# Retention two chunks at a time in a fused retention and maxout-FFN kernel

## The chip, the cores and the metric

The kernel runs on one core of a Trainium2 chip. The metric is device time in microseconds (us) of one execution; the figure given is the median of several runs. Engines are named as in the profile: PE is TensorE (matmul), PEld its weight loads, DVE is VectorE, ACT is ScalarE, POOL is GpSimd, SP is the queue that issues nearly all DMAs.

## The reference

The first half is retention, attention without a softmax: for 8 batches of 8 heads, 576 positions and 64 features,

```
scores = q @ k.T / sqrt(64)
ret    = scores * gamma_head ** (i - j)      (zero where j > i)
x      = ret @ v
```

with one gamma per head. The heads are put side by side, so x has 4608 rows of 512. The second half is a maxout FFN: h = max(x @ w1, x @ w2, x @ w3) with 768 hidden columns, and out = h @ w_out, 4608 x 512. q, k, v are float32; the weights come as 64-bit floats and are turned into float32 on the chip.

## The kernel before, in words

The 4608 rows are cut into 36 chunks of 128 rows (C) and 9 tiles of 512 rows (four chunks each, CPT). A batch has 576 rows, 4.5 chunks, so chunks 4, 13, 22 and 31 hold the end of one batch in their first 64 rows and the start of the next in the last 64; `start_of(g)` gives the row at which a new batch starts in chunk g, or None.

Retention goes by chunk. The decay is split into a factor for the keys (put on v by `decay_values`, on POOL), one for the queries (put on at the end), and a state that carries the earlier chunks of the same batch. For each chunk g there are these steps:

- `load(g)`: q, k and v from memory, all from SP. From chunk 7 on (BY_PE) q and a second copy of k (`kx`) are brought in blocks of 32 x 32 by 16 small DMAs each, so that VectorE's 32 x 32 transpose finishes the job; before that, q and k come whole and are transposed on PE. k and v in plain layout are one DMA each (two where the chunk crosses a batch).
- `transposes(g)` gives kT and qT, heads on partitions in pairs.
- `scores(g)`: 8 matmuls (L186), each with one head's 64 rows of the array, into two PSUM banks; VectorE masks them into `st` (L189). Then, still in `scores`, the state for the next chunk: 4 matmuls of k by decayed v (`kv`, L197), in chunks with a batch start at row 64 with those last 64 rows only; VectorE adds the old state (L200, L202) and POOL multiplies by the decay of a chunk (L203).
- `values(g)`: 8 matmuls of v by `st` (L216), each writing 64 partitions, then 4 of the state by qT (L221) into the same bank `o`, if the chunk has rows that continue a batch; VectorE applies the queries' decay on the way into `xT` (L223). After a tile's fourth chunk it and POOL also make the sums S that the FFN needs (L228 to L231).

[...] four in the ring `ps_r` (tag "r": kt, qt, scores, kv, o, in order of use), two in `ps_x` and two in `ps_y`.

The FFN (`ffn`) is a generator that yields after a unit. In tile 0 a unit is two plain matrix products (`up_plain`, L504), and between them the weights are converted by VectorE, ACT and POOL, step by step (`convert`); each converted piece issues the load of the piece six later (`load_weights`, L258 to L263) on SP, since six raw buffers exist. From tile 1 on a unit is `up`, seven products of half-size blocks (a Strassen-Winograd scheme, L446) with copies on ACT and sums on VectorE; nine units fill h, and `downs` (L319) makes the output in three further stretches, with four stores on SP (L333).

No scheduler reorders anything[...]. The main loop (L576 to L587) interleaves: for tile t, the twelve pieces of the FFN alternate with the steps of the four chunks of tile t + 1, one step before each piece: transposes (and, before it, the load of chunk g + 1), scores (and `decay_values(g + 1)`), values; then the next chunk. Chunks 0 to 3 are done in a prologue (L553 to L573).

Of the kernel before, what the change touches and what calls it, by code (L numbers as in the profile page):

```python
# [34 lines left out]
FP32 = mybir.dt.float32  # L35
# [4 lines left out]
ALU = mybir.AluOpType  # L40
PSUM = bass.MemoryType.PSUM

C = 128
NT = 4 * C
NH = NT // 2
BY_PE = 7
# [5 lines left out]
def kernel(  # L52
# [14 lines left out]
    nc = tc.nc  # L67
    P = 128
    B, H, S, D = q.shape
    N, DM = out.shape  # L70
    DF = moe_w1.shape[1]
    NP = H // 2
    NG = B * S // C
    NDC = DM // P
    NF = DF // P
    CPT = NT // C
# [3 lines left out]
    raw = ctx.enter_context(tc.tile_pool(name="raw", bufs=AHEAD + 1))  # L80
    vpool = ctx.enter_context(tc.tile_pool(name="vpool", bufs=3))
    att = ctx.enter_context(tc.tile_pool(name="att", bufs=2))
    stp = ctx.enter_context(tc.tile_pool(name="stp", bufs=2))
    xpool = ctx.enter_context(tc.tile_pool(name="xpool", bufs=2))
    spool = ctx.enter_context(tc.tile_pool(name="spool", bufs=1))
    hpool = ctx.enter_context(tc.tile_pool(name="hpool", bufs=1))
# [5 lines left out]
    ps_r = ctx.enter_context(tc.tile_pool(name="ps_r", bufs=4, space=PSUM))  # L92
# [5 lines left out]
    gq = const.tile([P, NP, C], FP32, name="gq")  # L98
# [17 lines left out]
    def start_of(g):  # L116
        r = -g * C % S
        return r if r < C else None

    masks = {0: causal, None: causal}  # L120
    for r in sorted({start_of(g) for g in range(NG)} - {0, None}):
        m = masks[r] = const.tile([C, C], FP32, name=f"causal{r}")
# [4 lines left out]
    raws, vds, qks, sts, states = {}, {}, {}, {}, {}  # L127

    def spans(g):

        row = 0
        while row < C:
            b, pos = divmod(g * C + row, S)
            n = min(C - row, S - pos)
            yield row, b, pos, n
            row += n

    def load(g, *between):
        rows = (("k", k), ("q", q), ("v", v)) if g < BY_PE else (("k", k), ("v", v))
        for n, src in () if g < BY_PE else (("q", q), ("kx", k)):  # L140

            t = raws[n, g] = raw.tile([P, NP, C // 32, 32], FP32, tag=n, name=n + "raw", bufs=3 if n == "q" else 2)
            for blk in range(C // 32):
                b, pos = divmod(g * C + 32 * blk, S)
                for a in range(4):
                    nc.sync.dma_start(
                        t[32 * a:32 * a + 32, :, blk, :],
                        src[b, a // 2::2, pos:pos + 32, 32 * (a % 2):32 * (a % 2) + 32].rearrange("p j i -> j p i"))
        for n, src in rows:
            if n == "v":  # L150
                for t, what in between:
                    nc.sync.dma_start(t[:], what)
            t = raws[n, g] = raw.tile([C, H, D], FP32, tag=n, name=n + "raw", bufs=4 if n == "k" else 3)
            for row, b, pos, m in spans(g):
                nc.sync.dma_start(t[row:row + m], src[b, :, pos:pos + m, :].rearrange("h p d -> p h d"))

    def decay_values(g):
        t = vds[g] = vpool.tile([C, H, D], FP32, tag="vd", name="vd")
        nc.gpsimd.tensor_tensor(t[:], raws.pop(("v", g))[:], gk[:].unsqueeze(2).to_broadcast([C, H, D]),  # L159
                                op=ALU.mult)  # L160

    def pair(t, p):
        return t[:, 2 * p:2 * p + 2, :].rearrange("a h d -> a (h d)")

    def transposes(g):
        both = qks[g] = {}
        if g >= BY_PE:
            for n in ("k", "q"):
                t = both[n] = att.tile([P, NP, C], FP32, tag=n + "T", name=n + "T", bufs=2 if n == "k" else 3)
                nc.vector.transpose(t[:].rearrange("a p c -> a (p c)"),  # L170
                                    raws.pop(("kx" if n == "k" else n, g))[:].rearrange("a p b i -> a (p b i)"))
            return
        for n, src in (("k", raws["k", g]), ("q", raws.pop(("q", g)))):
            pt = ps_r.tile([P, NP, C], FP32, tag="r", name=n + "t")
            for p in range(NP):
                nc.tensor.transpose(pt[:, p, :], pair(src, p), ident[:C, :C])
            t = both[n] = att.tile([P, NP, C], FP32, tag=n + "T", name=n + "T", bufs=2 if n == "k" else 3)
            nc.scalar.copy(t[:], pt[:])

    def scores(g):  # L180
        qT, kT = qks[g]["q"], qks[g]["k"]
        s = [ps_r.tile([C, NP, C], FP32, tag="r", name=f"s{j}") for j in range(2)]
        for p in range(NP):
            for j in range(2):
                r = slice(D * j, D * (j + 1))
                nc.tensor.matmul(s[j][:, p, :], lhsT=kT[r, p, :], rhs=qT[r, p, :], start=True, stop=True)  # L186
        st = sts[g] = att.tile([C, 2, NP, C], FP32, tag="st", name="st", bufs=2)
        for j in range(2):
            nc.vector.tensor_tensor(st[:, j], s[j][:], masks[start_of(g)][:].unsqueeze(1).to_broadcast([C, NP, C]),  # L189
                                    op=ALU.mult)  # L190
        kr = raws.pop(("k", g))
        if g + 1 == NG or start_of(g + 1) == 0:
            return
        r = start_of(g) or 0
        kv = ps_r.tile([P, NP, P], FP32, tag="r", name="kv")
        for p in range(NP):
            nc.tensor.matmul(kv[:, p, :], lhsT=pair(kr, p)[r:], rhs=pair(vds[g], p)[r:], start=True, stop=True)  # L197
        t = states[g + 1] = stp.tile([P, NP, P], FP32, tag="state", name="state")
        if start_of(g) is not None:
            nc.vector.tensor_tensor(t[:], kv[:], gs[:], op=ALU.mult)  # L200
        else:
            nc.vector.tensor_tensor(t[:], kv[:], states[g][:], op=ALU.add)  # L202
            nc.gpsimd.tensor_tensor(t[:], t[:], gs[:], op=ALU.mult)  # L203

    xT, xS = {}, {}

    def values(g):
        old = C if start_of(g) is None else start_of(g)
        t, i = divmod(g, CPT)
        if i == 0:  # L210
            xT[t] = xpool.tile([P, NDC, NT], FP32, tag="xT", name="xT")
        st, vr, qT = sts.pop(g), vds.pop(g), qks.pop(g)["q"]
        o = ps_r.tile([P, NP, C], FP32, tag="r", name="o")
        for p in range(NP):
            for j in range(2):
                nc.tensor.matmul(o[D * j:D * (j + 1), p, :], lhsT=vr[:, 2 * p + j, :], rhs=st[:, j, p, :],  # L216
                                 start=(p == 0), stop=(old == 0 and p == NP - 1), skip_group_check=True)
        if old > 0:
            sd = states.pop(g)
            for p in range(NP):  # L220
                nc.tensor.matmul(o[:, p, :old], lhsT=sd[:, p, :], rhs=qT[:, p, :old],  # L221
                                 start=False, stop=(p == NP - 1), skip_group_check=True)
        nc.vector.tensor_tensor(xT[t][:, :, i * C:(i + 1) * C], o[:], gq[:], op=ALU.mult)  # L223
        if i == CPT - 1 and t > 0:
            x = xT[t]
            a11, a12, a21, a22 = (x[:, 2 * d:2 * d + 2, NH * r:NH * (r + 1)] for r in range(2) for d in range(2))
            s1, s2, s3, s4 = (spool.tile([P, 2, NH], FP32, tag=f"S{n}", name=f"S{n}") for n in (1, 2, 3, 4))
            nc.vector.tensor_tensor(s1[:], a21, a22, op=ALU.add)  # L228
            nc.vector.tensor_tensor(s2[:], s1[:], a11, op=ALU.subtract)
            nc.gpsimd.tensor_tensor(s3[:], a11, a21, op=ALU.subtract)  # L230
            nc.gpsimd.tensor_tensor(s4[:], a12, s2[:], op=ALU.subtract)  # L231
            xS[t] = {1: a11, 2: a12, 3: s4[:], 4: a22, 5: s1[:], 6: s2[:], 7: s3[:]}
# [200 lines left out]
    def convert(n):  # L433
        for _ in range(n):
            next(converting, None)
# [119 lines left out]
    warm(2)  # L555
    decay_values(1)
    scores(0)
    transposes(1)
    values(0)
    decay_values(2)  # L560
    scores(1)
    transposes(2)
    values(1)
    decay_values(3)
    scores(2)
    transposes(3)
    convert(2)
    values(2)
    convert(2)
    scores(3)  # L570
    decay_values(4)
    convert(2)
    values(3)  # L573
    transposes(4)
    convert(4)
    for t in range(N // NT):  # L576
        work = ffn(t)
        for g in range((t + 1) * CPT, (t + 2) * CPT):
            for step in (transposes, scores, values):
                if g < NG:  # L580
                    if step is transposes and g + 1 < NG:
                        load(g + 1)
                    if step is scores and g + 1 < NG:
                        decay_values(g + 1)
                    if g > CPT or step is not transposes:
                        step(g)
                next(work, None)  # L587


# [49 lines left out]
```

## Time and profile before

| what | value |
|---|---|
| median of 13 runs | 830.18 us (828.86 to 834.15) |
| profiled execution, its own time | 829.92 us |
| its span | 828.2 us |
| PE busy | 822.5 us |
| DVE, POOL, ACT busy | 432.4, 190.4, 173.7 us |
| retention matmuls: scores L186, values L216, state L221, kv L197 | 41.8, 39.8, 36.9, 36.6 us of listed time |
| small q and kx DMAs | 464 each, 16 KB |

The span is the program's own stretch of the trace, about 1.7 us shorter than the execution's time. A group's listed time counts overlapping instructions in full, so the four retention rows add up to more than the stretch they fill. Every matmul stands in the trace as two records. In the chain of waits each record is charged from the end of the one before it to its own end, so its lengths add up to elapsed time.

### The profile page before, as it was taken

The numbers are of one execution on the slowest core, as the hardware profiler recorded it, in microseconds if no ns is written. First come the engines' busy times: TensorE is split into PE (matmuls) and PEld (weight loads), VectorE is DVE, ScalarE is ACT, GpSimd is POOL, SyncE is SP. The second block draws the span as 40 slices with busy tenths as digits, with TensorE's granted clock in tenths as the row PEclk, the third lists the DMA queues.
The fourth block names the chain that finished last, engine by engine and source line by source line (L and its number), as shares of the span: only waits on it lengthen the run. The fifth ranks groups of instructions, "written<-read, shape, count | busy, mean of one in ns | idle before, by whom it ended". The sixth has DMA issues, their size and how long they took to land.

```text
span 828.2 us, 12659 instructions
## 1 busy us (share of the span) xinstructions
PE 822.5 (99%) x4616; PEld 668.7 (81%) x4616; DVE 432.4 (52%) x805; ACT 173.7 (21%) x401; POOL 190.4 (23%) x182
## 2 busy tenths in 40 slices
PE   9999999999999999999999999999999999999998
PEld 8555547888888888888888888888888888888887
DVE  4999886455455544544454445444544435433342
ACT  3766511111111111110111111111111011111211
POOL 3644565212111120113011211111111202101000
PEclk9999999999999999999999999999999999999999
DMA  9964431343133323332233323341333233201001
GB/s 236 296 173 152 103 71 45 57 79 63 51 56 55 57 79 57 56 57 57 56 62 70 62 53 57 56 78 60 56 58 54 59 71 63 46 13 39 1 1 51
DMA packets 236094, 59.33 MB, mean 72 GB/s; under 512 B 217088, under 2 KB 234496, under 8 KB 236032
## 3 DMA queue, kind: packets, MB, share of 16 engines
q1 hardware_dynamic: 235888, 58.53, 31.4%
q8 instruction: 36, 0.59, 0.3%
q14 instruction: 26, 0.21, 0.1%
q10 hardware_dynamic: 144, 0.00, 0.0%
HBM read 49.03 MB, written 9.44 MB: 71 GB/s over the span
## 4 chain that ended last, share of the span: by engine, by line
PE 88%; DVE 5%; issue 2%; ACT 2%; DMA 1%; POOL 0%; SPq 0%; DVEq 0%; ACTq 0%
PE x L446 30%; PE z L446 15%; PE dx L319 10%; PE y L446 8%; PE dz L319 5%; PE s L186 4%; PE o L216 4%; PE kv L197 4%; PE o L221 4%; PE dy L319 3%; PE down L495 2%; DVE expo L398 1%; DVE frac L387 1%; DVE expo L382 1%; DVE mant L393 1%
## 5 line engine op out<-in xcount | busy, mean ns | idle before, releaser
L446 PE MATMUL x<-S,T 128*128 128x256 f32 x576 | 148.0, 379 | 0.0
L159 POOL TENSOR_TENSOR vd<-vraw,gk 128x512 f32<-128x512 f32 x36 | 38.3, 1063 | 364.2 <-DMA vraw<-in_v_dram 358.0
L446 PEld LDWEIGHTS x<-S,T 128*128 128x128 f32 x576 | 109.0, 190 | 15.6 <-ACT u L451 0.3
L446 PE MATMUL x<-xT,w 128*128 128x256 f32 x288 | 74.8, 382 | 0.0
L476 DVE TENSOR_TENSOR tmp<-x,p 128x256 f32<-128x256 f32 x48 | 20.4, 425 | 103.5 <-PE x L446 103.5
L446 PE MATMUL x<-S,w 128*128 128x256 f32 x288 | 74.3, 381 | 0.0
L446 PE MATMUL z<-S,w 128*128 128x256 f32 x288 | 73.9, 379 | 0.0
L446 PE MATMUL z<-xT,T 128*128 128x256 f32 x288 | 73.9, 379 | 0.0
L446 PE MATMUL y<-xT,w 128*128 128x256 f32 x288 | 73.9, 379 | 0.0
L451 ACT COPY p<-x 128x256 f32<-128x256 f32 x72 | 26.8, 372 | 220.2 <-PE x L446 220.2
L189 DVE TENSOR_TENSOR st<-s,causal 128x512 f32<-128x512 f32 x72 | 46.3, 685 | 41.6 <-PE s L186 41.6
L504 PE MATMUL up<-xT,w 128*128 128x512 f32 x144 | 63.5, 594 | 0.2 <-POOL w L404 0.2
L446 PEld LDWEIGHTS z<-S,w 128*128 128x128 f32 x288 | 54.7, 190 | 7.4
L446 PEld LDWEIGHTS y<-xT,w 128*128 128x128 f32 x288 | 54.7, 190 | 7.4
L446 PEld LDWEIGHTS z<-xT,T 128*128 128x128 f32 x288 | 54.5, 189 | 7.7
L223 DVE TENSOR_TENSOR xT<-o,gq 128x512 f32<-128x512 f32 x36 | 24.9, 691 | 68.0 <-PE o L221 61.5
L446 PEld LDWEIGHTS x<-S,w 128*128 128x128 f32 x288 | 49.3, 189 | 13.3 <-issue 1.5
L446 PEld LDWEIGHTS x<-xT,w 128*128 128x128 f32 x288 | 51.5, 190 | 6.6 <-issue 0.8
L297 POOL TENSOR_TENSOR H<-h 128x256 f32<-128x256 f32 x24 | 18.0, 749 | 148.0 <-DVE h L489 148.0
L504 PEld LDWEIGHTS up<-xT,w 128*128 128x128 f32 x144 | 26.7, 190 | 30.7 <-issue 29.9
L465 DVE TENSOR_TENSOR tmp<-y,p 128x256 f32<-128x256 f32 x48 | 20.4, 425 | 52.8 <-PE y L446 52.8
L451 ACT COPY u<-x 128x256 f32<-128x256 f32 x72 | 26.8, 372 | 100.1 <-PE x L446 95.8
(92 smaller groups left out, 1229.2 us busy)
## 6 DMA issues: line engine op xcount, KB each, us to landing
bits<-in_moe_w_dram SPq DMA_DIRECT2D x18, 512.0 KB, 5.1
out_dram<-osb SPq DMA_DIRECT2D x35, 256.0 KB, 2.1
kraw<-in_k_dram SPq DMA_DIRECT2D x32, 256.0 KB, 3.0
vraw<-in_v_dram SPq DMA_DIRECT2D x32, 256.0 KB, 3.4
qraw<-in_q_dram SPq DMA_DIRECT2D x464, 16.0 KB, 1.8
kxraw<-in_k_dram SPq DMA_DIRECT2D x464, 16.0 KB, 1.8
bits<-in_moe_w_out_dram SPq DMA_DIRECT2D x6, 512.0 KB, 3.9
qraw<-in_q_dram SPq DMA_DIRECT2D x6, 256.0 KB, 4.6
```

What stands on the lines that cost most here:

```text
L159: nc.gpsimd.tensor_tensor(t[:], raws.pop(("v", g))[:], gk[:].unsqueeze(2).to_broadcast([C, H, D]), op=ALU.mult)
L186: nc.tensor.matmul(s[j][:, p, :], lhsT=kT[r, p, :], rhs=qT[r, p, :], start=True, stop=True)
L189: nc.vector.tensor_tensor(st[:, j], s[j][:], masks[start_of(g)][:].unsqueeze(1).to_broadcast([C, NP, C]), op=ALU.mult)
L197: nc.tensor.matmul(kv[:, p, :], lhsT=pair(kr, p)[r:], rhs=pair(vds[g], p)[r:], start=True, stop=True)
L216: nc.tensor.matmul(o[D * j:D * (j + 1), p, :], lhsT=vr[:, 2 * p + j, :], rhs=st[:, j, p, :], start=(p == 0), stop=(old == 0 and p == NP - ...
L221: nc.tensor.matmul(o[:, p, :old], lhsT=sd[:, p, :], rhs=qT[:, p, :old], start=False, stop=(p == NP - 1), skip_group_check=True)
L223: nc.vector.tensor_tensor(xT[t][:, :, i * C:(i + 1) * C], o[:], gq[:], op=ALU.mult)
L319: nc.tensor.matmul(out[m], lhsT=hS[n](fp)[:, m * P:(m + 1) * P], rhs=late["T"][n][:, fp, :], start=first and fp == 0 and (m == 0 or last a ...
L446: nc.tensor.matmul(out[:], lhsT=w[:, d * P:(d + 1) * P], rhs=xS[t][n][:, d, :], start=first and d == 0, stop=d == 1, skip_group_check=True)
L451: nc.scalar.copy(c[:], src[:])
L465: nc.vector.tensor_tensor(c11, y[:], p1[:], op=ALU.add)
L504: nc.tensor.matmul(ps[:], lhsT=w_sb[i, fb][:, dc * P:(dc + 1) * P], rhs=xT[t][:, dc, :], start=(dc == 0), stop=(dc == NDC - 1))
```

## The change

`scores` is split: the state part becomes a step `state(g)` of its own. `values` takes several chunks: first the L216 matmuls of all of them, then the L221 matmuls of each with its read-out. `stp`, the ring of states, has three buffers instead of two. `load` gets a part `load_blocks` that issues the small DMAs of chosen blocks of a chunk.

The main loop is replaced by a table of twelve steps, `steps(t)`. From the second of these tables on, chunks a and b go together: transposes of a and the load of a + 2; transposes of b; scores of a and of b in a row and the load of b + 2; state of a; state of b; values of a and b; then the same for the next two. For chunks 4 to 7, which run beside the first tile's FFN and its weight conversion, the table is written out: scores 4 and state 4 stay together between the first two units, scores 5 stand alone, values 4 and 5, scores 6 and 7, values 6 and 7 are in a row, and the small DMAs of chunks 7, 8 and 9 are spread over the steps in blocks.

```diff
-    stp = ctx.enter_context(tc.tile_pool(name="stp", bufs=2))
+    stp = ctx.enter_context(tc.tile_pool(name="stp", bufs=3))
...
-    def load(g, *between):
-        rows = (("k", k), ("q", q), ("v", v)) if g < BY_PE else (("k", k), ("v", v))
-        for n, src in () if g < BY_PE else (("q", q), ("kx", k)):
-
-            t = raws[n, g] = raw.tile([P, NP, C // 32, 32], FP32, tag=n, name=n + "raw", bufs=3 if n == "q" else 2)
-            for blk in range(C // 32):
+    def load_blocks(g, *blocks):
+        for n, src in (("q", q), ("kx", k)):
+
+            if 0 in blocks:
+                raws[n, g] = raw.tile([P, NP, C // 32, 32], FP32, tag=n, name=n + "raw", bufs=3 if n == "q" else 2)
+            t = raws[n, g]
+            for blk in blocks:
...
+    def load(g, *between):
+        if g >= BY_PE and ("q", g) not in raws:
+            load_blocks(g, *range(C // 32))
+        for n, src in (("k", k), ("q", q), ("v", v)) if g < BY_PE else (("k", k), ("v", v)):
...
+    def state(g):
+
         kr = raws.pop(("k", g))
         if g + 1 == NG or start_of(g + 1) == 0:
             return
...
+    def values(*chunks):
+
+
+        def before(g):
+            return C if start_of(g) is None else start_of(g)
+
+        o = {g: ps_r.tile([P, NP, C], FP32, tag="r", name="o") for g in chunks}
+        for g in chunks:
+            st, vr = sts.pop(g), vds.pop(g)
             for p in range(NP):
-                nc.tensor.matmul(o[:, p, :old], lhsT=sd[:, p, :], rhs=qT[:, p, :old],
-                                 start=False, stop=(p == NP - 1), skip_group_check=True)
-        nc.vector.tensor_tensor(xT[t][:, :, i * C:(i + 1) * C], o[:], gq[:], op=ALU.mult)
+                for j in range(2):
+                    nc.tensor.matmul(o[g][D * j:D * (j + 1), p, :], lhsT=vr[:, 2 * p + j, :], rhs=st[:, j, p, :],
+                                     start=(p == 0), stop=(before(g) == 0 and p == NP - 1), skip_group_check=True)
+        for g in chunks:
+            t, i = divmod(g, CPT)
+            qT, old = qks.pop(g)["q"], before(g)
+            if old > 0:
+                sd = states.pop(g)
+                for p in range(NP):
+                    nc.tensor.matmul(o[g][:, p, :old], lhsT=sd[:, p, :], rhs=qT[:, p, :old],
+                                     start=False, stop=(p == NP - 1), skip_group_check=True)
+            if i == 0:
+                xT[t] = xpool.tile([P, NDC, NT], FP32, tag="xT", name="xT")
+            nc.vector.tensor_tensor(xT[t][:, :, i * C:(i + 1) * C], o[g][:], gq[:], op=ALU.mult)
...
+    def steps(t):
...
+        if t == 1:
+            a, b, c, d = range(CPT, 2 * CPT)
+            at(0, (load, b))
+            at(1, (scores, a), (state, a))
+            at(2, (transposes, b), (decay_values, b), (load, c))
+            at(3, (scores, b), (load_blocks, d, 0))
+            at(4, (state, b), (load_blocks, d, 1, 2))
+            at(5, (values, a, b), (load_blocks, d, 3), (load, d))
+            at(6, (transposes, c), (decay_values, c), (load_blocks, d + 1, 0))
+            at(7, (transposes, d), (decay_values, d), (load_blocks, d + 1, 1, 2))
+            at(8, (scores, c), (scores, d), (load_blocks, d + 1, 3), (load, d + 1))
+            at(9, (state, c), (load_blocks, d + 2, 0, 1))
+            at(10, (state, d), (load_blocks, d + 2, 2))
+            at(11, (values, c, d), (load_blocks, d + 2, 3), (load, d + 2))
+            return todo
+        for n in range(0, CPT, 2):
+            a, b, m = CPT * t + n, CPT * t + n + 1, 6 * (n // 2)
+            at(m, (transposes, a), (decay_values, a), (load, a + 2))
+            at(m + 1, (transposes, b), (decay_values, b))
+            at(m + 2, (scores, a), (scores, b), (load, b + 2))
+            at(m + 3, (state, a))
+            at(m + 4, (state, b))
+            at(m + 5, (values, a, b))
+        return todo
+
     for t in range(N // NT):
         work = ffn(t)
-        for g in range((t + 1) * CPT, (t + 2) * CPT):
-            for step in (transposes, scores, values):
-                if g < NG:
-                    if step is transposes and g + 1 < NG:
-                        load(g + 1)
-                    if step is scores and g + 1 < NG:
-                        decay_values(g + 1)
-                    if g > CPT or step is not transposes:
-                        step(g)
-                next(work, None)
+        for todo in steps(t + 1):
+            for step in todo:
+                step()
+            next(work, None)
```

In the prologue each `scores(g)` is followed by `state(g)`, which leaves its order as it was.

More of the change, by code (lines that the diff above doesn't have):

```diff
@@ L148, in load @@
                         src[b, a // 2::2, pos:pos + 32, 32 * (a % 2):32 * (a % 2) + 32].rearrange("p j i -> j p i"))
-        for n, src in rows:
+    def load(g, *between):
+        if g >= BY_PE and ("q", g) not in raws:
+            load_blocks(g, *range(C // 32))
+        for n, src in (("k", k), ("q", q), ("v", v)) if g < BY_PE else (("k", k), ("v", v)):
             if n == "v":
@@ L205 @@
     xT, xS = {}, {}
[L207 to L219, printed above, removed]
-            for p in range(NP):
-                nc.tensor.matmul(o[:, p, :old], lhsT=sd[:, p, :], rhs=qT[:, p, :old],
-                                 start=False, stop=(p == NP - 1), skip_group_check=True)
-        nc.vector.tensor_tensor(xT[t][:, :, i * C:(i + 1) * C], o[:], gq[:], op=ALU.mult)
+    def values(*chunks):
[4 more added lines that the diff above has]
+            st, vr = sts.pop(g), vds.pop(g)
+            for p in range(NP):
+                for j in range(2):
[12 more added lines that the diff above has]
+            nc.vector.tensor_tensor(xT[t][:, :, i * C:(i + 1) * C], o[g][:], gq[:], op=ALU.mult)
         if i == CPT - 1 and t > 0:
@@ L557 @@
     scores(0)
+    state(0)
     transposes(1)
@@ L561 @@
     scores(1)
+    state(1)
     transposes(2)
@@ L565 @@
     scores(2)
+    state(2)
     transposes(3)
@@ L570 @@
     scores(3)
+    state(3)
     decay_values(4)
@@ L575, with at @@
     convert(4)
+    def steps(t):
+        todo = [[] for _ in range(3 * CPT)]
+        def at(n, *what):
+            todo[n].extend(partial(step, *args) for step, *args in what if args[0] < NG)
+        if t == 1:
[22 more added lines that the diff above has]
+        return todo
     for t in range(N // NT):
         work = ffn(t)
-        for g in range((t + 1) * CPT, (t + 2) * CPT):
-            for step in (transposes, scores, values):
-                if g < NG:
-                    if step is transposes and g + 1 < NG:
-                        load(g + 1)
-                    if step is scores and g + 1 < NG:
-                        decay_values(g + 1)
-                    if g > CPT or step is not transposes:
-                        step(g)
-                next(work, None)
+        for todo in steps(t + 1):
+            for step in todo:
+                step()
+            next(work, None)
 _INS = ['q', 'k', 'v', 'moe_w1', 'moe_w2', 'moe_w3', 'moe_w_out']
```

## The prediction

> **What bounds the kernel now.** I read the page first, then TensorE's waits, then the chain of waits in a middle tile, then the queues of the first tile.
>
> ```profile
> PE 822.5 (99%) x4616; PEld 668.7 (81%) x4616; DVE 432.4 (52%) x805; ACT 173.7 (21%) x401; POOL 190.4 (23%) x182
> ...
> PE 88%; DVE 5%; issue 2%; ACT 2%; DMA 1%; POOL 0%; SPq 0%; DVEq 0%; ACTq 0%
> ```
>
> TensorE is busy for 822.5 of 828.2 us. Who waits for whom, TensorE alone, is short:
>
> ```profile
> PE o L216 <- DVE st L189: 0.6, 2, 0.4
> PE s L186 <- ACT qT L178: 0.2, 1, 0.2
> PE up L504 <- POOL w L404: 0.2, 1, 0.2
> ```
>
> With 2.6 us of waits in all, no earlier load and no other buffer can win much: only less work on TensorE can. So I asked what each block costs, from the chain in 300 to 345 us (start, length, instruction, records; a matmul has two records):
>
> ```profile
> 299.95 0.34 PE o L221 x3
> ...
> 314.16 1.09 PE s L186 x16
> 315.25 1.09 PE kv L197 x8
> 316.34 0.86 PE x L446 x4
> ...
> 322.38 1.02 PE o L216 x16
> 323.41 1.09 PE o L221 x8
> 324.50 0.87 PE x L446 x4
> ...
> 336.59 1.09 PE s L186 x16
> 337.68 1.06 PE x L446 x4
> 338.74 0.86 PE y L446 x4
> ```
>
> The FFN's four records take 0.86. Straight after scores (337.68, a chunk with no kv) the same four take 1.06: 0.20 more. After kv (316.34) they take 0.86, but kv itself takes 1.09 for 8 records where the steady pitch of such records is 0.34/3 = 0.112, so 0.90: 0.19 more. Leaving the scores costs about 0.195, whoever comes next. Entering them costs as much: cut at 337.2 us, the chain gives 0.64 for the first 7 score records, so 0.45 for the last 9, four pairs and a bit, 0.112 a pair; eight pairs are 0.90 and the block took 1.09, so 0.195 went to the entry. Likewise L216: 0.47 for its first 5 records, 0.55 for the last 11, 0.109 a pair, 0.87 in all, so 0.15 for the entry; and L221 behind it pays 0.19 for leaving. One chunk's retention pays 0.39 around its scores and 0.345 around its values.
>
> Scores use 64 rows of the array and L216 64 columns, everything else 128x128. The test is a chunk whose kv has 64 rows too (chunk 13, in 244 to 252 us):
>
> ```profile
> 246.82 1.09 PE s L186 x16
> 247.91 0.89 PE kv L197 x8
> 248.81 1.06 PE x L446 x4
> ```
>
> Here kv pays nothing after the scores, and the FFN block behind it pays the 0.20. The price is for changing the shape of the tile.
>
> [...] my blocks run from end to end, and all lengths but those at a change of shape repeat to 0.01 us, so I use them.
>
> **The change, part by part.** *Scores in a row, values in a row.* In tiles 1 to 7 chunks 8 to 35 form 14 pairs; of chunks 4 to 7 the values pair twice and the scores once (6, 7). That is 15 merged score blocks and 16 merged value blocks. Each merge takes away one entry and one exit: 15 x 0.39 = 5.85 us and 16 x 0.345 = 5.5 us. No other record goes or comes. The seam inside a merged block (scores of one chunk, then of the next) isn't in the trace of before. Bounds: a gain has no source, since the pitch inside a block is already steady[...]. I take 0, since the shape stays.
>
> *States on their own.* kv now stands between FFN units; with 128 rows its shape is theirs and it costs 8 x 0.112. But chunks 13, 22 and 31 cross a batch after 64 rows: their kv was next to the scores and shared their shape, and now changes shape twice more: 3 x 0.39 = 1.2 us lost. Chunk 4 also has 64 rows, but its scores and state stay together.
>
> *Four score banks at once.* They take all four ps_r buffers. Two of them last held the values of the pair before, read by VectorE three units (18 us) earlier; the kv one unit later needs a bank whose mask is done. Masks: four at 0.69 listed, about 2.5 us with their overlap. They start when the first chunk's scores end, 0.9 us before the second's, so they end some 1.7 us into the next unit, when its y (0.2 + 2 x 0.86) is just ready for VectorE; even 1 us late they are covered, as the next matmul that needs VectorE in that unit is product 3, five products on. VectorE is busy for 42 of 88 us in such a tile. Cost 0; without the cover up to 2.5 us a pair. The two read-outs of values in a row (2 x 0.69) hide in the same way, and at a tile's end under the four products (10 us) that still follow; GpSimd's S sums end there 6 us or more before they are used now (392.8 against 400).
>
> *Loads two chunks ahead.* SP issues the 34 DMAs of a chunk in 17.5 us (16 for q in about 8.2, 16 for k in 8.4, then 0.4 and 0.5), four chunks in 70 us of a tile of 88, and then waits for the stores (from 379.68 to 397.12 in that tile). SP's order inside a tile stays: four loads, four stores. k's transposed-load buffers are two, so chunk a + 2 can be loaded only when a is transposed, which is done at that same step; SP reaches those DMAs 8 us later, behind q's. In the tile's third load this may be a wait of 1 to 2 us; what stands behind it are loads due three units on and stores whose buffer is wanted 10 us later. Cost 0. As before, stores pace SP, and lag doesn't pile up: loads and four issues (2.5 us) are 73 of a tile of 86.5.
>
> *The first tile.* Here weights are converted on VectorE and SP also brings the weights:
>
> ```profile
> 68.89 8.86 SPq L260 DMA_DIRECT2D bits<-in_moe_w_out_dram  x4
> 77.87 8.58 SPq L146 DMA_DIRECT2D qraw<-in_q_dram  x16
> 86.50 7.55 SPq L146 DMA_DIRECT2D kxraw<-in_k_dram  x16
> ...
> 95.25 1.40 SPq L260 DMA_DIRECT2D bits<-in_moe_w_out_dram  x2
> ```
>
> The last two w_out pieces are queued behind chunk 7's 32 small DMAs; VectorE idles 2.48 us for them at 98.5, and the first down block takes 6.08 us where the second takes 5.32: 0.76 of stall. The change puts chunk 7's loads ahead of them in blocks of 8 and 16, mostly where SP was waiting for freed weight buffers (61.6 to 76.2 us), and only one block of chunk 8 (8 DMAs, 4.3 us) just before these two, so they leave at about 83 to 85 and land by 91. VectorE loses its 2.48 of idling, but before the last conversion it now does chunk 7's transposes (1.4) and masks (1.3) and no longer chunk 6's state add (0.7): 0.5 earlier in all, so the last w_out is there at 108.9 instead of 109.4. TensorE comes to it with 0.9 more (scores of 7) and 0.35 less (values of 4 and 5): it wants the last piece at 104.65 + 0.55 + 10 x 0.43 = 109.5. No stall: 0.76 gained. Bounds: that, and, if the DMAs stay late and VectorE ends 2.0 later, a stall of 1.8, so 1.1 lost. SP carries chunk 9's loads here too, 17.5 us, in time freed at 97 to 116.
>
> Sum: -5.85 - 5.5 + 1.2 - 0.76 = -10.9 us. The profiled execution took 829.92 (span 828.2 and 1.7 around it), 0.26 below the median of 830.18: 829.92 - 10.9 = 819.0, and in terms of the median 819.2.
>
> **The rivals.** [...] 5.6 back, 824.8. For it: nothing shown. Against: inside a block the matmuls already change bank and row half at 0.11 a pair. This is also the case in which the change doesn't do what it says. *The first tile takes some back:* w_out or VectorE late by 2 to 3 us, with the masks of two chunks and chunk 7's transposes in a stretch where VectorE is 100% busy (62 to 83 us): 821 to 822. Against: from the fifth matmul group on weights stand ready 5 to 14 us before use and the PSUM buffers 8. *The banks bind, slower:* the second chunk's scores wait for VectorE to read the banks of the values before, or the next unit waits behind four masks. It decides from 10.9/14 = 0.78 us a pair; with a full pair of masks (1.29) exposed in 15 pairs it would be 819.2 + 19.4 = 838.6. Against: the 18 us between the values and the next scores.
>
> **How the numbers follow.** Chances: forecast 0.70, with its own range 817 to 821 (the medians' noise, some tenths to 1 us, and pitches off by 0.02); first tile 0.12; seam 0.12; banks 0.05; the rest 0.01. From 816.5 to 823 lie the forecast nearly whole and the first tile: 0.8. A no-change within 0.2% (1.7 us) would need the gain lost almost exactly: 0.02. Slower: the banks, 0.05. Faster: 0.93.
>
> **What would show it.** Right: score groups of 32 records in about 1.99 us and value groups of 32 in about 1.9; kv with 128 rows 0.90 and, thrice, 64-row kv with 0.39 around it; TensorE's waits no longer than now; tiles of 86.5 where they were 88; the first down block at 5.2. Wrong: any wait of TensorE for masks or values in tiles 1 to 7, a jump at the 17th record of a merged block, waits of VectorE for q or k loads, or weight waits in the first 110 us.

## The result and the profile after

The changed kernel takes 820.36 us (median of 7 runs, 820.01 to 820.62) against 830.51 us (32 runs) for the kernel before: 0.9874 of it, 95% interval 0.9861 to 0.9886, so 1.3% or about 10.2 us faster. The profiled execution took 820.62, its span 818.9 where it was 828.2.

On the page, TensorE is as full as it was, but busy for 10.2 us less with the same 4616 records. So the price of the changes of shape had stood in its busy time, not in its idle time:

```profile
PE 812.3 (99%) x4616; PEld 671.0 (82%) x4616; DVE 433.6 (53%) x805; ACT 173.8 (21%) x401; POOL 190.9 (23%) x182
```

Its waits (engine, line, who was waited for: us, times, longest) have grown a little, from 2.6 to 3.6 us in all, and all of them lie in the prologue and the first tile:

```profile
...
PE o L226 <- DVE st L194: 1.0, 2, 0.8
PE down L510 <- POOL w_out L419: 0.8, 1, 0.8
...
```

The chain of waits in 300 to 350 us (start, length, what, records) shows a pair of chunks; the line numbers of the retention matmuls are now L191 (scores), L205 (kv), L226 (values), L234 (state by qT), and the FFN's is L461:

```profile
317.62 1.99 PE s L191 x32
319.60 1.06 PE x L461 x4
...
325.84 0.89 PE kv L205 x8
326.73 0.87 PE x L461 x4
...
338.82 1.90 PE o L226 x32
340.72 1.98 PE o L234 x16
342.70 0.86 PE x L461 x4
```

32 score records take 1.99 where two blocks of 16 took 2.18, and only one block behind them is 0.20 too long where there were two. kv costs 0.89 where it cost 1.09. Values take 1.90 + 1.98 for two chunks where they took 4.22. Nothing happens at the 17th record: the block is one entry and a steady pitch of its 16 pairs of records, 0.195 + 16 x 0.112 = 1.99. From the first FFN unit of tile 1 to the last matmul's end the trace has 695.1 us before and 685.8 after, 9.3 less. The first tile gave nothing in this pair of profiles: tile 1 begins at 130.16 us in both. The chains of the two, in 90 to 132 us, show why. TensorE's first block of output products (`down`) waits for the last piece of w_out, before:

```profile
109.44 1.12 PE down L495 x2
...
120.02 10.30 PE down L495 x24
```

and after:

```profile
108.97 1.13 PE down L510 x2
...
120.02 10.30 PE down L510 x24
```

The piece comes 0.47 us earlier, but 0.48 us more of retention now stands behind it (4.77 where it was 4.29), so both reach the third block at the same time.

The stretch from tile 1 to the end repeats to 0.1 us in three profiles of the changed kernel (685.77, 685.77, 685.85). Of the 10.2 us between the medians, 9.3 are in this stretch. The other 0.9 then lies ahead of tile 1, where these three profiles differ by 1.1 us.

### The profile page after: what moved, and what is told of

Same layout as the page of the kernel before. It is cut to its first block, busy times and chain, and to the rows that moved or that the text cites. A ratio compares the mean times of both kernels' runs of the same rounds, so it can differ in the third digit from the quotient of the medians.

```text
span 818.9 us, 12678 instructions
## 1 busy us (share of the span) xinstructions
PE 812.3 (99%) x4616; PEld 671.0 (82%) x4616; DVE 433.6 (53%) x805; ACT 173.8 (21%) x401; POOL 190.9 (23%) x182
## 4 chain that ended last, share of the span: by engine, by line
PE 88%; DVE 6%; issue 2%; DMA 2%; ACT 1%; SPq 1%; POOL 0%; DVEq 0%; POOLq 0%
PE x L461 31%; PE z L461 15%; PE dx L334 10%; PE y L461 8%; PE dz L334 5%; PE s L191 4%; PE o L226 4%; PE o L234 3%; PE kv L205 3%; PE dy L334 3%; PE down L510 2%; DVE expo L413 2%; DVE frac L402 1%; DMA qraw<-in_q_dram 1%; DVE mant L408 1%
## 5 line engine op out<-in xcount | busy, mean ns | idle before, releaser
L461 PE MATMUL x<-S,T 128*128 128x256 f32 x576 | 147.9, 379 | 0.0
L461 PEld LDWEIGHTS x<-S,T 128*128 128x128 f32 x576 | 109.1, 190 | 15.4 <-ACT u L466 0.3
L211 POOL TENSOR_TENSOR state<-state,gs 128x512 f32<-128x512 f32 x24 | 32.2, 1340 | 241.2 <-DVE state L210 241.2
L461 PE MATMUL x<-xT,w 128*128 128x256 f32 x288 | 75.6, 385 | 0.0
L461 PE MATMUL x<-S,w 128*128 128x256 f32 x288 | 74.3, 381 | 0.0
L461 PE MATMUL y<-xT,w 128*128 128x256 f32 x288 | 73.9, 379 | 0.0
L461 PE MATMUL z<-S,w 128*128 128x256 f32 x288 | 73.9, 379 | 0.0
L461 PE MATMUL z<-xT,T 128*128 128x256 f32 x288 | 73.9, 379 | 0.0
L312 POOL TENSOR_TENSOR H<-h 128x256 f32<-128x256 f32 x24 | 20.6, 857 | 226.9 <-DVE h L504 226.9
L461 PEld LDWEIGHTS z<-S,w 128*128 128x128 f32 x288 | 54.7, 190 | 7.4
L461 PEld LDWEIGHTS y<-xT,w 128*128 128x128 f32 x288 | 54.7, 190 | 7.4
L461 PEld LDWEIGHTS z<-xT,T 128*128 128x128 f32 x288 | 54.5, 189 | 7.7
L461 PEld LDWEIGHTS x<-S,w 128*128 128x128 f32 x288 | 49.3, 189 | 13.3 <-issue 1.5
L461 PEld LDWEIGHTS x<-xT,w 128*128 128x128 f32 x288 | 52.1, 190 | 8.0 <-issue 0.5
```

The source lines that it names most:

```text
L312: chores.append(lambda: (pool(s3, a11, a21, op=ALU.subtract), pool(s4, a12, s2, op=ALU.subtract)))
L461: nc.tensor.matmul(out[:], lhsT=w[:, d * P:(d + 1) * P], rhs=xS[t][n][:, d, :], start=first and d == 0, stop=d == 1, skip_group_check=True)
```

## The experiments

Ratios are to the kernel before, timed beside each experiment. The changed kernel was timed again beside two groups of them.

**Values apart.** The same work at the same places, but each chunk's values finished before the next one's:

```diff
-            at(m + 5, (values, a, b))
+            at(m + 5, (values, a), (values, b))
```

> Edit: in the pairs of chunks 8 to 35 the values of a and then of b, each with its L221 matmuls, at the same place in the order; all loads, scores and states as in the changed kernel (820.4). Theory [...]: 14 more exits and entries, 14 x (0.196 + 0.15) = 4.8 us, so 825.2; in the chain L216 and L221 alternate at 1.02 and 1.09 where they took 1.90 and 1.98 for two. Rival (the gain came from loads and steps placed earlier): 820.4, blocks no longer than before. Rival [...]: 821 to 823.

Measured: 825.02 us, ratio 0.991 (0.9887 to 0.9933). From tile 1 to the end 690.2 us, 4.4 more than in the changed kernel. The chain of this kernel, values of a pair:

```profile
340.40 1.02 PE o L226 x16
341.43 1.09 PE o L234 x8
342.52 1.02 PE o L226 x16
343.54 1.09 PE o L234 x8
```

The pair takes 4.22, against 3.88. In pair (18, 19) chunk 18 has no rows that continue a batch, so nothing of another shape stands between its values and those of 19: 13 x 0.346 = 4.5 is the theory's figure when that is seen. The loads were the same as in the changed kernel, so they don't explain the loss, and 4.4 us of 4.5 is the price nearly whole: 825.02 lies above the 821 to 823 of the last rival.

**Scores apart.** The state of a back between the two scores:

```diff
-            at(m + 2, (scores, a), (scores, b), (load, b + 2))
-            at(m + 3, (state, a))
+            at(m + 2, (scores, a), (state, a), (scores, b), (load, b + 2))
```

> Edit: state of a stands between the scores of a and of b, in chunks 8 to 35; else as the changed kernel (820.4). Theory: 11 pairs have a 128-row kv between their scores and pay one more exit and entry, 11 x 0.39 = 4.3 us; pairs (8, 9) and (26, 27) have no kv of a and stay merged; in pair (22, 23) the 64-row kv now stands between two blocks of its own shape and saves 0.39. In sum +3.9, so 824.3. Rival (loads and steps): 820.4. Rival (scores in a row cost by their PSUM banks): faster than 820.4, since the four banks are now taken more slowly.

Measured: 824.16 us, ratio 0.9906 (0.9878 to 0.9934); from tile 1 to the end 689.9, 4.1 more. Its chain has three blocks, each with a change of shape in front:

```profile
317.84 1.09 PE s L191 x16
318.93 1.09 PE kv L205 x8
320.02 1.09 PE s L191 x16
```

**Both apart,** both edits in one kernel, the loads, the table and the first tile still those of the change:

> Edit: both of the former edits. All loads two chunks ahead, the step table and the first tile stay as in the changed kernel. Theory: the two add, 4.8 + 3.9 = 8.7, so 829.1, within 1.5 us of the kernel before (830.5): nearly all of the gain was shape changes and the loads bring nothing. Rival (loads): some 820 to 825.

Measured: 829.32 us, ratio 0.9971 (0.9958 to 0.9983); from tile 1 to the end 694.4, 8.6 more, the sum of the two (8.5). With most merges of tiles 1 to 7 undone, nearly the whole gain is gone although all loads still go two chunks ahead. What is left, 0.3%, holds the first tile's part too. From tile 1 to the end only 0.7 us is left (694.4 against 695.1), and that is not the loads' either: two pairs of scores and one of values are still merged here, and with the kv of 22, 13 and 31 at their new places there are four changes of shape fewer than before, worth 0.74 by the price.

The count can be made for every kernel, since the trace gives the rows and columns of each record. The price is the one read from the kernel before, 0.15 us into the 64-column shape and 0.195 for every other change:

| kernel | changes of shape from tile 1 on | their price, us | tile 1 to the end, us | without the price |
|---|---|---|---|---|
| before | 112 | 20.6 | 695.1 | 674.5 |
| changed | 62 | 11.5 | 685.8 | 674.3 |
| values apart | 88 | 16.0 | 690.2 | 674.3 |
| scores apart | 82 | 15.4 | 689.9 | 674.5 |
| both apart | 108 | 19.8 | 694.4 | 674.5 |

What remains is the same to 0.3 us in all five, although the loads go one chunk ahead in the first and two in the others. So count and price explain the stretch, and nothing is left for the loads. In the three kernels at the end of this section, which merge more (56, 55 and 49 changes), 674.8, 674.5 and 675.0 remain: there a change saved brought somewhat less than its price.

**First tile in the old order,** the rest changed. Run twice, the second time beside the changed kernel:

```diff
-            at(1, (scores, a), (state, a))
-            at(2, (transposes, b), (decay_values, b), (load, c))
-            at(3, (scores, b), (load_blocks, d, 0))
...
+            at(1, (scores, a), (state, a), (decay_values, b))
+            at(2, (values, a))
+            at(3, (load, c), (transposes, b))
...
+            at(6, (load, d), (transposes, c))
...
+            at(11, (values, d), (load, d + 2))
```

> Edit: the table for chunks 4 to 7 has the order of the kernel before (one chunk at a time, chunk 7's loads in front of the last two w_out loads, chunk 9's loads at its end); chunks 8 to 35 as in the changed kernel (820.4). Theory (the first tile is paced by VectorE's weight conversion, and what TensorE saves there comes back as a wait for w_out): 820.0 to 820.9, and the first FFN unit of tile 1 starts at 130 us as in both kernels. Rival (the prediction's sum for the first tile, 1.1 of merges and 0.76 of stall): 822.2.

> The changed kernel again, for comparison on the same chip: 820.1, tile 1 beginning at 129.2 to 130.4.

> Edit: first tile in the order of the kernel before, the rest changed, now timed beside the changed kernel. Theory (the first tile's own part of the change is lost to the wait for w_out): within 0.5 us of the changed kernel, with more wait at the first down block where chunk 7's loads stand ahead of the last w_out. Rival (the prediction's 1.9 us for that tile): 1.9 us slower.

Measured: 821.72 us the first time, ratio 0.988 (0.9852 to 0.9907), and 821.35 the second, ratio 0.989 (0.9877 to 0.9904), beside 820.47, ratio 0.988 (0.9867 to 0.9894), for the changed kernel. So the new first tile is worth about 0.9 us in the medians, with intervals that overlap; neither the theory's "within 0.5" nor the rival's 1.9. The start of tile 1 moves from run to run: in nine profiles with the new table it lies between 129.2 and 130.4 us; with the old order it lies at 130.2 (the kernel before) and 131.4, and at 134.1 in an execution that ran 2.8 us over its kernel's median. In that one TensorE idled 2.3 us in one go at the first down block, and its granted clock averaged 0.998 over the span, where it was 1.000 in the three other executions. In the second run the chain in 96 to 124 us goes through the late transfer:

```profile
96.43 5.74 DMA bits<-in_moe_w_out_dram
...
109.38 1.28 POOL w_out L419
...
110.69 1.13 PE down L510 x2
```

**First tile, chunk 7 behind the weights.** In the changed kernel the same place looks like this (chain in 99 to 122 us):

```profile
99.74 2.39 DVE st L194 x4
...
106.06 1.52 DVE expo L413
...
107.65 1.28 POOL w_out L419
...
108.97 1.13 PE down L510 x2
```

No transfer is in it: the last two w_out loads are issued at 84.97 us instead of 95.25. VectorE's own work, four masks among it, now sets the end. So chunk 7's transposes and the scores of 6 and 7 were moved behind the conversion, and in a second version the state of 7 too:

```diff
-            at(7, (transposes, d), (decay_values, d), (load_blocks, d + 1, 1, 2))
-            at(8, (scores, c), (scores, d), (load_blocks, d + 1, 3), (load, d + 1))
-            at(9, (state, c), (load_blocks, d + 2, 0, 1))
-            at(10, (state, d), (load_blocks, d + 2, 2))
-            at(11, (values, c, d), (load_blocks, d + 2, 3), (load, d + 2))
+            at(7, (load_blocks, d + 1, 1, 2))
+            at(8, (load_blocks, d + 1, 3), (load, d + 1))
+            at(9, (transposes, d), (decay_values, d), (state, c), (load_blocks, d + 2, 0, 1))
+            at(10, (scores, c), (scores, d), (load_blocks, d + 2, 2))
+            at(11, (state, d), (values, c, d), (load_blocks, d + 2, 3), (load, d + 2))
```

(In the first version `(state, d)` stands at 10, behind the scores.)

> The changed kernel itself, for comparison on the same chip. 820.4, or 9.3 to 10.5 us under the kernel before on this chip; first FFN unit of tile 1 at 129 to 130.5 us.

> Edit: in the first tile, transposes of chunk 7 move from the step before unit 7 to the step after unit 8, and scores of 6 and 7 to one step later still, so that VectorE does neither the two transposes (1.3 us) nor the four masks (2.5 us) before the last weight pieces. Loads stay. Theory (the first tile is paced by VectorE's conversion): the last w_out is ready 3.8 us earlier, TensorE comes to the first down block 2.0 us earlier, the block's wait for w_out (1.4 us) goes, and about as much is gained: tile 1 begins at about 129, some 1 us under the changed kernel in the same call. Rival (the masks behind the weight sums come late and the values of 6 and 7 wait for them): no gain, with a wait of TensorE for masks at L226 of 1 us or more. Rival (w_out is paced by its own transfer): the wait at the first down block stays.

> Edit: as in the former try, transposes of 7 and scores of 6 and 7 come behind the last weight pieces, but the state of 7 one step later still, ahead of the values of 6 and 7, so that its kv no longer needs a bank whose mask is queued behind the weight sums. Theory (the lost 5 us were that one wait, and the first tile is paced by the conversion): no wait of TensorE over 1 us there, the first down block at 5.8 instead of 6.6, tile 1 beginning 0.5 to 1 us earlier than in the changed kernel, some 0.7 us under it in time. Rival (TensorE meets the masks at the values instead): 1 us or more of waiting at L226, no gain.

First version: 826.33 us, ratio 0.9944 (0.9931 to 0.9956), beside 820.07, ratio 0.9873 (0.9858 to 0.9889), for the changed kernel: 6.3 us slower, against the theory, and the wait is not at L226, where the rival had put it. Its timeline:

```profile
106.61 2.06 PE L191 MATMUL s<-qT,kT 64*128 64x128 f32 x32
...
111.65 2.47 DVE L194 TENSOR_TENSOR st<-s,causal 128x512 f32<-128x512 f32 x4
...
112.43 2.05 PE L205 MATMUL kv<-vd,kraw 128*128 128x128 f32 x8 [3.77 <-POOL w L442]
```

The two chunks' scores fill all four banks of the ring; the next user, kv of 7, needs the first bank, whose mask stood behind weight sums on VectorE until 111.65 us. kv starts at 112.43, when the first of the four masks (2.47 for all) is through; the row names a GpSimd instruction that ended at about the same time and has nothing to do with kv. TensorE idled 3.8 us, its granted clock averaged 0.94 over 100 to 130 us (1.00 over the 100 us ahead of that and the 90 us behind it), and these eight kv records took 2.05 where they take 1.05. The wait and the slower kv are some 5 us (3.8 + 1.0); the profiled execution took 825.07, the fastest of five, and what made the others up to 1.4 us longer was not looked at. This is the wait of the prediction's slower rival ("the banks bind"), in a place where VectorE is late.

Second version: 820.03 us, ratio 0.9874 (0.9861 to 0.9888), beside 820.47. The masks still come at 111.46, but nothing asks for their banks before 113.6. Its chain in 96 to 122 us:

```profile
101.25 5.21 PE down L510 x12
106.47 1.99 PE s L191 x32
108.45 5.35 PE down L510 x12
```

The first down block takes 5.21 instead of 6.56 and tile 1 begins at 128.7, earlier than in any other profile. That fits a wait made by VectorE, but it is one profile: with the first tile as in the changed kernel, eight of nine profiles had 5.88 to 6.94 for this block and one, in the kernel with scores apart, 5.19. From tile 1 to the end this kernel took 686.1, 0.4 longer, and the 0.4 us in the medians are in the noise. A gain is not shown.

**The 64-row kv with its own kind.** The state of chunks 13, 22 and 31 straight ahead of the pair's scores:

```diff
+            half = [g for g in (a, b) if start_of(g) == C // 2]
-            at(m + 2, (scores, a), (scores, b), (load, b + 2))
-            at(m + 3, (state, a))
-            at(m + 4, (state, b))
+            at(m + 2, *((state, g) for g in half), (scores, a), (scores, b), (load, b + 2))
+            at(m + 3, *((state, g) for g in (a,) if g not in half))
+            at(m + 4, *((state, g) for g in (b,) if g not in half))
```

> Edit: the state of chunks 13, 22 and 31 (kv with 64 rows, the shape of the scores) goes straight ahead of the two chunks' scores; else as the changed kernel. Theory: two changes of shape less in three pairs, 3 x 0.39 = 1.2 us under the changed kernel, the kv at 0.90 plus the entry of 0.2 and the scores of 32 records at 1.79. Rival (kv now takes the fourth bank, which the second chunk's scores need 2 us later, and VectorE's read of it isn't done): up to 0.8 us lost in each of the three, so no gain or 1 us slower.

Measured: 819.62 us, ratio 0.9863 (0.985 to 0.9877), beside 820.07; from tile 1 to the end 685.05, 0.72 less. Kv of 13 in the changed kernel, in its chain:

```profile
244.11 1.09 PE kv L205 x8
245.20 1.06 PE x L461 x4
```

The kv takes 0.20 more than its pitches and the FFN block behind it 0.20 more: the 0.39 a piece which the prediction charged for these three. Moved, it gives back 0.24 a piece: kv and scores together took 3.02 (228.71 to 231.73 us in its chain) where one entry and the pitches, 0.195 + 8 x 0.112 + 16 x 0.112 = 2.88, were expected. The 0.14 over was not followed up. TensorE waits for no bank there.

**Values beside scores.** L221's work ahead of L216's inside `values`, and in tiles 1 to 7 the first pair's values straight ahead of the second pair's scores (with a fourth buffer for qT and decayed v and two for raw v):

```diff
-            at(m + 2, (scores, a), (scores, b), (load, b + 2))
...
-            at(m + 5, (values, a, b))
+            before_them = [] if n == 0 else [(values, a - 2, a - 1)]
+            at(m + 2, *before_them, (scores, a), (scores, b), (load, b + 2))
...
+            if n > 0:
+                at(m + 5, (values, a, b))
```

> Edit: in values the L221 matmuls come ahead of the L216 ones, and in tiles 1 to 7 the values of the first pair move to just ahead of the scores of the second (three units later), so that the 64-column shape is followed directly by the 64-row one; qT and decayed v get a fourth buffer, raw v two instead of three. Theory (the price is per change of shape): of four changes around these two blocks three are left, 7 x 0.2 = 1.4 us under the changed kernel. Rival (a direct change between two partial shapes costs as much as two): no gain. Rival (the second chunk's scores wait for the read-out of the values' banks): TensorE waits for VectorE at the scores, up to 0.7 us in 7 places, so up to 3.5 us slower.

Measured: 818.67 us, ratio 0.9855 (0.9842 to 0.9869); from tile 1 to the end 684.6, 1.2 less than the changed kernel's 685.8. A pair in its chain:

```profile
181.19 0.89 PE o L227 x8
182.08 1.90 PE o L233 x32
183.98 1.99 PE s L191 x32
185.96 1.06 PE x L462 x4
```

The state's matmuls pay nothing behind the FFN, and the scores pay the same 0.195 behind the 64-column block as behind a 128x128 one: the direct change between these two partial shapes counts as one, and one of four is saved. Seven times 0.195 would be 1.4 us; the trace has 1.2, with one FFN block 0.3 us too long ahead of this first pair, at 180 us, behind a sum of VectorE.

**Both of the last two:**

> Edit: values of a tile's first pair straight ahead of the second pair's scores, and the 64-row kv of 13, 22 and 31 straight ahead of their scores. Theory: the two gains add, 1.2 and 0.7 between the start of tile 1 and the end, so 683.9 there against 685.8 in the changed kernel, and some 818.2. Rival (with kv, values and scores together TensorE waits for PSUM banks in pairs (22, 23) and (30, 31)): no better than 818.7.

Measured: 817.96 us, ratio 0.9847 (0.9834 to 0.9861), beside 820.47: from tile 1 to the end 683.88, where 683.9 was expected. It is the fastest of all, 2.5 us under the changed kernel and 12.3 under the kernel before, timed beside it.

## Why the prediction was right, and where it was not

The forecast was 819.2 in 816.5 to 823; measured 820.36. By its steps:

- *Price of a change of shape: right.* 0.15 to 0.20 each. Undoing the merges one at a time gave 4.4 and 4.1 us against 4.5 and 3.9 by that price, and both 8.6 against 8.4. The runs show the price and that it goes with the change of shape; they don't show what TensorE does in that time.
- *Tiles 1 to 8: right.* 14 pairs by 0.39 + 0.345, less 1.2 for the three 64-row kv, is 9.1 to 9.2; the trace has 9.3. The 1.2 is shown by the kv rows; without that term the sum would have been a good 1 us too high.
- *The seam costs nothing: right.* 1.99 for 32 records; the rival of 5.6 us (31 merges by 0.18), in which a merged block pays once more at its seam, falls.
- *Banks and masks: right in tiles 1 to 8.* No wait of TensorE there (none in 131 to 818 us of the changed kernel). What the rival expected showed in one run: with VectorE some 4 us behind on the masks in the first tile, TensorE waited 3.8 us, and the kv behind the wait took 2.05 us instead of 1.05.
- *Loads two chunks ahead cost nothing in tiles 1 to 8: right.* They bring nothing there either: the 0.7 us that the kernel with both blocks apart keeps is the price of four changes of shape. That the loads could have stayed one chunk ahead under the new order was not tried.
- *The first tile: wrong.* The prediction took 1.1 of merges and 0.76 of vanished wait. The transfer did come 10 us earlier and the last w_out was ready at 108.93, where 108.9 had been worked out. The weight was thus ready when forecast, and the step that failed is "TensorE comes to it with 0.9 more (scores of 7) and 0.35 less (values of 4 and 5)": it left out that the values of chunk 6, 2.1 us, also go from ahead of the down block to behind it. TensorE therefore came at 103.5 and not at 105.2 (not at 103.1, since its waits for masks in the prologue were 0.4 us longer in this profile), and the block's stall is 1.4 (6.56 against 5.15) instead of 0.76, not zero. What was saved on TensorE ahead of that point came back as waiting for a weight that VectorE had not finished. Such a wait for w_out in the first 110 us is one of the signs that the prediction itself had named for being wrong. Of the 1.9 us nothing shows in the first two profiles and about 0.9 in the medians of the kernels timed side by side.

So the sum closes: 9.3 us from tile 1 on, where 9.1 had been forecast, and about 0.9 in the first tile instead of 1.9, are the 10.2 us between the medians, where 10.9 had been forecast. The rest of the 1.2 us between 819.2 and 820.36 is the kernel before, whose median over 32 runs is 0.3 above the 830.18 that the forecast started from. The 0.9 rests on medians whose intervals overlap.

## What to carry to other kernels

When TensorE is full and waits for nobody, take the chain of waits and divide each block by its records: a block that is longer than its steady pitch, or a block of another kind whose length depends on its predecessor, may be paying for a change of tile shape (0.15 to 0.20 us each in this kernel); count the changes, and order the work so that blocks of one shape stand together. A merged block asks for more PSUM banks at once (the scores here four instead of two), so look at who uses the ring next, and whether the engine that empties it is on time at that place. And in a stretch that another engine paces, count every instruction that crosses the waiting point in either direction before booking a gain there.

## What the runs showed that was not expected

- Changing straight from the 64-column to the 64-row shape cost 0.195 us (1.99 for 32 score records, in the chain of values beside scores), no more than changing between 64 rows and 128x128.
- Moved straight ahead of the scores, the 64-row kv block overlaps with them in the trace: in the chain, from 229.46 to 229.79 us, the last three kv records alternate with the first three of the scores, although the program emits all of kv first. The two together were still 0.14 us longer than their entry and pitches.
- In the profile in which TensorE idled 3.8 us in one go at the end of the first tile (chunk 7 behind the weights, first version), its granted clock averaged 0.94 over 100 to 130 us and 1.00 ahead of and behind that; over the whole span it was 0.996 to 0.998 in all five executions of that kernel. In the profile with 2.3 us of idling in one go (the first tile in the old order, first run) it was 0.998 over the span, and 1.000 in the three other executions, which were 2.5 to 3.2 us shorter. In the profiles of the kernel before and of the changed kernel TensorE waited 0.8 us at most at that place, and the clock over 100 to 130 us was 1.00. That the idling caused the drop was not tested.
